# Spare TensorE products between the last key comparisons, with new weight homes, half-wise expert products and a new order of the first ticks

## The chip, the cores and the metric

The kernel runs on one core of one Trainium2 chip. The metric is device time in microseconds of one execution. Before the change three runs took 322.2, 322.96 and 324.96 us.

## The reference

The reference is a causal attention with a window of 128 positions and 4 sink positions (batch 4, 8 heads, 768 positions, head size 64), followed by a mixture of 8 experts with a capacity of 80 tokens each:

```
scores = q @ k.T / sqrt(64);  keep = sink | (0 <= i - j < 128)
x      = softmax(scores where keep) @ v            # 3072 rows of 512
logits = x @ w_gate;  expert = argmax;  gate = softmax(logits)[expert]
for e in range(8):
    tok = tokens of e; if more than 80: the 80 with the largest gate
    out[tok] = gate[tok] * (relu(x[tok] @ w1[e]) @ w2[e])   # w1 512x1024, w2 1024x512
```

All other rows of `out` are zero. All data is 32-bit floating point.

## The kernel before

**Attention.** A tick handles two units, each a pair of heads for one block of 128 queries. There are 48 ticks: four batches with 12 ticks each. In tick n the kernel issues the scores of tick n (`scores`, TensorE), masks and maxima (`softmax`, VectorE), the exponentials (`exps`, L541, ScalarE), and for tick n-1 the transposes of the probabilities (`transposes`), their copy out of PSUM (`keep_probs`, L569), the two masked copies on GpSimd (`own_probs`, `before_probs`), and for tick n-2 the weighted sums (`weighted`) and their copy (`keep_x`). The order on each engine is written out by hand: the loop calls these functions in a fixed order, and a calendar (`at`, `run`) adds further work at named places of a tick ("act mid", "pool", "dve end" and so on). The sink rows of `v` are rounded on ScalarE (`round_v`, L382) and the rest of the rounding is kept by GpSimd (`split_v`, L387); for batch 0 this happens in tick 1.

**Gate and ranks.** Each finished block of rows is turned, scaled and stored to `x_rows` in DRAM on the SP queue (L645; the last two on ScalarE's queue). Its gate gives one key for a token, and the kernel ranks tokens by comparing every key with all keys: VectorE compares pieces of 768 keys (`rank_compare`, L746 and L749), TensorE counts the columns of the results (`rank_count`, L763, and `rank_count_last`, L773). Comparisons that are left when attention ends run one after the other on VectorE. The column sums go through `owed` (L939), `off` (ScalarE), `ot` (GpSimd) and `os` (VectorE, L952). At the end `hot` (L983) marks the slots of the 80 tokens of each expert, 24 products give `pi` (L986), and the indices drive eight gathers from `x_rows` on GpSimd's DMA queue (L1007). Beside them TensorE runs 14 products of 480 columns into an unused bank (L1005).

**Experts.** For each expert the kernel transposes the gathered rows (`tokens`, L1037, copied by L1039), multiplies by w1 (`ffn1`, 128 products into `ph`, L1051), rectifies on ScalarE, multiplies by w2 (`ffn2`, 128 products into `py`, L1066), transposes back (`rows`, L1082) and scatters to `out`. The order is ffn1(0), ffn1(1), ffn2(0), ffn1(2), ffn2(1) and so on. In `ffn1` the four chunks c of the inner dimension run innermost, in `ffn2` the eight chunks k; a product addresses 64 columns of a weight tile (`columns`).

**Weights.** There are 32 weight tiles of 1024 KB, half a matrix each, loaded on the SP queue in the order of their use (`load_weight`, L293). The first 17 have homes of their own: NA = 6 loaded in ticks 26 to 41, every third tick; NB = 7 in the space of the q, k and v tiles (`ld`), which is closed after the last tick; NC = 4 in the space of the attention's working tiles (`wk`: probabilities, their copies, row blocks, comparison results). Tile 17 + k takes the home of tile 1 + 7k//4, so its load waits until the products of that tile are done. For the copies into unused output rows, `zeros` is written 24 times from tick 4 on.

Of the kernel before, what the change touches and what calls it, by code (L numbers as in the profile page):

```python
# [20 lines left out]
E, F = 8, 1024  # L21
# [211 lines left out]

Z0, ZD, W0, WD = 4, 1, 26, 3
NPB = NBLK // 2
NSPLIT = 1
SROWS = 16 * SINK
# [4 lines left out]
def attention_moe(ctx: ExitStack, tc, q, k, v, n_sink, window, w_gate, w1, w2, capacity, q_t, k_t, v_t, vs_t, wg_t, out):  # L244
# [4 lines left out]
    dram = ctx.enter_context(tc.tile_pool(name="dram", bufs=1, space=DRAM))  # L249
    fast = ctx.enter_context(ExitStack())  # L250

    NA, NB, NC = 6, 7, 4
    wpool = fast.enter_context(tc.tile_pool(name="wpool", bufs=NA))

    x_rows = dram.tile([NT, DM], F32, name="x_rows")
# [28 lines left out]
    def load_weight():  # L284
        n = len(wtiles)
        which, e, half = wsrc[n]
        src = (w1, w2)[which][e].rearrange("(g c p) f -> g p c f", g=2, p=P)[half]

        k = n - NA - NB - NC
        in_home.append(n if k < 0 else in_home[1 + 7 * k // 4])  # L290
        pool, m = homes[in_home[n]]
        t = pool.tile([P, 2 * F], F32, tag=f"w{m}", name=f"w_{which}_{e}_{half}", bufs=1)
        nc.sync.dma_start(t.rearrange("p (c f) -> p c f", c=src.shape[1]), src)  # L293
        wtiles[(which, e, half)] = t

    zeros = const.tile([P, DM], F32, name="zeros")
    ve.memset(zeros, 0.0)

    with ExitStack() as actx:
        wk = actx.enter_context(tc.tile_pool(name="wk", bufs=2))  # L300
# [54 lines left out]
        def load_q(g, pieces=1):  # L355
            qs[g] = ld.tile([P, NPAIR, 2 * P], F32, tag="q", name=f"q_{g}", bufs=3)
            n = NPAIR // pieces
            for i in range(pieces):
                nc.sync.dma_start(qs[g][:, i * n:(i + 1) * n], q_t[g // NPB, g % NPB][:, i * n:(i + 1) * n])

        def load_k(b, pieces=1):
            ks[b] = ld.tile([P, NPAIR, NBLK * BLKW], F32, tag="k", name=f"k_{b}")
            n = NPAIR // pieces
            for i in range(pieces):
                nc.sync.dma_start(ks[b][:, i * n:(i + 1) * n], k_t[b][:, i * n:(i + 1) * n])

        def load_v(b, upto=NPB):

            if b not in vv:
                vst[b] = vst_rows[b % 2]  # L370
                vv[b] = ld.tile([P, NBLK, DM], F32, tag="v", name=f"v_{b}")
# [8 lines left out]
        def round_v(b, m):  # L380
            a, hp = m // 2, slice(m % 2 * 2, m % 2 * 2 + 2)
            ac.copy(vst[b][0:SROWS, a, hp].bitcast(F32R), vst_raw[0:SROWS, a, hp])  # L382

        def split_v(b, m):

            a, hp = m // 2, slice(m % 2 * 2, m % 2 * 2 + 2)
            po.tensor_tensor(vst[b][32:SROWS, a, hp].bitcast(F32R), vst_raw[32:SROWS, a, hp], vst[b][32:SROWS, a, hp],  # L387
                             ALU.subtract)

        def scale_q(g, parts=1):  # L390
# [4 lines left out]


        first_q = qs[0] = ld.tile([P, NPAIR, 2 * P], F32, tag="q", name="q_0", bufs=3)
        first_k = ks[0] = ld.tile([P, NPAIR, NBLK * BLKW], F32, tag="k", name="k_0")
        for i in range(NPAIR):
            nc.sync.dma_start(first_q[:, i], q_t[0, 0][:, i])  # L400
            nc.sync.dma_start(first_k[:, i, 0:2 * BLKW], k_t[0][:, i, 0:2 * BLKW])
# [385 lines left out]
            at(Z0 + ZD * n, nc.sync.dma_start, out[n * P:(n + 1) * P, :], zeros)  # L787
        for n in range(NA):
            at(W0 + WD * n, load_weight)
        at((2, "pool"), make_experts)  # L790
        at((3, "pool"), make_picks)
        at((4, "pool"), make_ties)
# [3 lines left out]
        for b in range(B):  # L796
            s = b * NPB * NPAIR
            if b + 1 < B:
                at(s + 4, load_v, b + 1)
                at(s + 5, load_k, b + 1)  # L800
                for m in range(4):
                    at((s + 6 + m, "act end"), round_v, b + 1, m)
                    at((s + 7 + m, "pool"), split_v, b + 1, m)
        for m in range(4):
            at((1, "act mid"), round_v, 0, m)
            at((1, "pool"), split_v, 0, m)
        for g in range(2, NG):
            at((g - 2) * NPAIR + 1, load_q, g)
        for g in range(1, NG):
# [47 lines left out]
        with tc.manual_schedule():  # L857
            n = 0
            while n <= END:
                now[0] = n  # L860
                if n < NTK:
                    scores(n)
                t = n - 1 if 0 <= n - 1 < NTK else None
                if t is not None:
                    sink_probs(t)
                run(n, "dve early")
                run(n, "act early")
                if t is not None:
# [12 lines left out]
                run(n, "dve mid")  # L881
                if t is not None and n >= NTK:
                    own_probs(t)
                    before_probs(t)
                run(n, "pool")
                if t is not None:
                    if n < NTK:
                        own_probs(t)
                        before_probs(t)
                    sinks_keep(t)  # L890
                if 0 <= n - 2 < NTK:
                    weighted(n - 2)
                    keep_x(n - 2)
                run(n, "pe end")
                run(n, "act end")
                run(n, "dve end")
                run(n, "pool end")
                left = len(rank_todo)
                for _ in range(min(left, 3) if n >= NTK else -(-left // 3)):
                    rank_compare()  # L900
                run(n)
                if n == END:

                    lctx.close()
                    wpool2 = fast.enter_context(tc.tile_pool(name="wpool2", bufs=1, side="right", reuse_waits="tile"))
                    homes += [(wpool2, m) for m in range(NB)]
                    for _ in range(NB):
                        load_weight()
                n += 1

            now[0] = n
            i = NTILE - 1
# [44 lines left out]
            while rank_todo:  # L957
                rank_compare()
                rank_count_last(last)
            ve.tensor_tensor(colacc[:, 0:i], colacc[:, 0:i], last[:, 0:i], ALU.subtract)  # L960
            assert not cal and not rank_done, cal

    with ExitStack() as fctx:
# [77 lines left out]
        def ffn1(e):  # L1041
            need(0, e)
            x = xts.pop(e)
            h = wk.tile([P, HC, CAP], F32, tag="h", name=f"h_{e}")
            for half in range(2):
                ph = ps_h.tile([P, HC // 2, CAP], F32, tag="ph", name=f"ph_{e}_{half}")
                for f in range(HC // 2):
                    fc = half * (HC // 2) + f
                    for c in range(DC):
                        for m in range(2):  # L1050
                            pe.matmul(ph[m * D:(m + 1) * D, f], columns(0, e, c, fc * P + m * D),  # L1051
                                      x[:, c], start=(c == 0), stop=(c == DC - 1), skip_group_check=True)
                ac.activation(h[:, half * (HC // 2):(half + 1) * (HC // 2)], ph, AF.Relu)  # L1053
            hs[e] = h

        def ffn2(e, between=None):
            need(1, e)
            h = hs.pop(e)
            yts[e] = wk.tile([P, DC, CAP], F32, tag="yt", name=f"yt_{e}")
            py = ps_y.tile([P, DC, CAP], F32, tag="py", name=f"py_{e}")  # L1060
            last = ps_h.tile([P, HC // 2, CAP], F32, tag="ph", name=f"py2_{e}") if e == E - 1 else py
            for dc in range(DC):
                to = py if dc < DC // 2 else last
                for k in range(HC):
                    for m in range(2):
                        pe.matmul(to[m * D:(m + 1) * D, dc], columns(1, e, k, dc * P + m * D), h[:, k],  # L1066
                                  start=(k == 0), stop=(k == HC - 1), skip_group_check=True)
# [106 lines left out]
```

## Time and profile before

| what | value |
|---|---|
| runs | 322.2, 322.96, 324.96 us |
| profiled execution | 321.46 us, span 319.7 us |
| TensorE busy | 276.4 us (86%) |
| VectorE busy | 180.5 us (56%) |
| ScalarE busy | 159.1 us (50%) |
| GpSimd busy | 164.8 us (52%) |
| mean granted TensorE clock | 0.953 |
| DMA | 69.72 MB, mean 218 GB/s |
| weight loads | 32 of 1024 KB, median 6.7 us from issue to landing |

The span runs from the first to the last instruction of one profiled execution; the time of that execution is a little longer. Busy shares are averages over stages: the attention fills about the first 195 us, the last comparisons and the choice of tokens follow until about 222 us, the experts take the rest. The granted clock is the share of TensorE's full 2.4 GHz; 0.50 is 1.2 GHz.

### The profile page before, as it was taken

To read this page: it belongs to the slowest core of one execution; us is meant where nothing else is said; L and a number is where in the kernel's file an instruction comes from. 1 tells how busy PE (TensorE), PEld (TensorE's weight loads), DVE (VectorE), ACT (ScalarE), POOL (GpSimd) and SP (SyncE) were. 2 spreads that over 40 slices of the span, in tenths; PEclk is the share of its full clock that TensorE was granted. 3 is DMA by queue.
4 is the path that set the end of the run, shared out by engine and by line. 5 is a ranking of instruction groups with operands and counts; after the bars stand their busy time and mean duration, and the time that the engine had idled before them with its cause. 6 is when DMAs were issued, how large, how long until landed. Compare 5 with 4: busy or idle time off the path is not lost. (4 is left out here: it accounts for less than half of the span.)

```text
span 319.7 us, 11526 instructions
## 1 busy us (share of the span) xinstructions
PE 276.4 (86%) x4616; PEld 218.6 (68%) x4616; DVE 180.5 (56%) x576; ACT 159.1 (50%) x631; POOL 164.8 (52%) x365
## 2 busy tenths in 40 slices
PE   7498999999979999999999895745888989999792
PEld 2265776867767777777676673332788989998681
DVE  5345988777888989799989999970000000000001
ACT  0766897788968788777776661100111212111110
POOL 4396797769897588967667765507300111011001
PEclk9679999999999999999999999558999999999998
DMA  6999143699553899345260002999996696677501
GB/s 180 326 310 413 73 133 134 223 285 324 201 202 113 279 380 408 133 148 156 111 200 35 35 3 73 355 408 368 321 380 238 220 351 211 214 253 267 186 23 49
DMA packets 27115, 69.72 MB, mean 218 GB/s; under 512 B 2736, under 2 KB 3760, under 8 KB 26672
## 3 DMA queue, kind: packets, MB, share of 16 engines
q1 hardware_dynamic: 25744, 65.78, 59.5%
q0 software_dynamic: 1024, 2.62, 2.5%
q8 instruction: 38, 0.62, 0.8%
q10 hardware_dynamic: 288, 0.52, 0.4%
q14 instruction: 21, 0.17, 0.2%
HBM read 55.02 MB, written 13.89 MB: 216 GB/s over the span
## 5 line engine op out<-in xcount | busy, mean ns | idle before, releaser
L541 ACT ACTIVATE prob<-sc,nm 128x132 f32<-128x132 f32 (+1 forms) x192 | 69.0, 376 | 6.6 <-DVE nm L531 6.4
L504 PE MATMUL sc<-k,q 64*64 64x196 f32 (+2 forms) x768 | 48.4, 341 | 11.4 <-ACT prob L541 10.0
L1094 POOL DMA_INDIRECT out_dram<-y,idx x8 | 7.4, 921 | 81.8 <-ACT y L1083 71.6
L569 ACT COPY pt<-pp 128x512 f32<-128x512 f32 x48 | 28.1, 586 | 32.7 <-PE pp L557 24.1
L1039 DVE COPY xs<-px 128x320 f32<-128x320 f32 x8 | 3.9, 492 | 70.4 <-PE px L1037 70.4
L531 DVE TENSOR_REDUCE nm<-sc 128x2 f32<-128x264 f32 (+1 forms) x96 | 41.4, 431 | 3.3
L1051 PE MATMUL ph<-xs,w 128*64 128x80 f32 x1024 | 38.6, 233 | 5.2 <-issue 4.0
L524 DVE COPY_PREDICATED sc<-upper,sc 128x256 f32<-128x256 int8 x80 | 33.7, 421 | 14.0 <-PE sc L504 7.2
L504 PEld LDWEIGHTS sc<-k,q 64*64 64x64 f32 x768 | 21.6, 135 | 29.1 <-ACT prob L541 20.9
L1051 PEld LDWEIGHTS ph<-xs,w 128*64 128x64 f32 x1024 | 36.8, 137 | 6.4 <-issue 5.5
L1066 PE MATMUL py<-h,w 128*64 128x80 f32 x1024 | 38.4, 234 | 2.7 <-issue 2.0
L541 ACT ACTIVATION_READ_ACCUMULATOR prob<-sc,nm 128x1 f32 x192 | 40.3, 210 | 0.0
L1066 PEld LDWEIGHTS py<-h,w 128*64 128x64 f32 x1024 | 36.3, 137 | 4.9 <-issue 4.0
L598 PE MATMUL xp<-pt,v 128*64 128x128 f32 x384 | 37.5, 288 | 0.0
L577 POOL TENSOR_SCALAR_AFFINE_SELECT own<-pt 128x512 f32<-128x512 f32 (+1 forms) x48 | 28.7, 598 | 16.1 <-ACT pt L569 15.5
L749 DVE TENSOR_SCALAR_CACHE_REDUCE gt<-krow,keys 128x768 bf16<-128x768 f32 x36 | 35.5, 1004 | 0.0
L557 PE MATMUL pp<-ident,prob 128*128 128x128 f32 x192 | 32.3, 292 | 0.0
L598 PE MATMUL xp<-own,v 128*64 128x128 f32 x320 | 31.3, 274 | 0.0
L557 PEld LDWEIGHTS pp<-ident,prob 128*128 128x128 f32 x192 | 20.8, 144 | 13.9 <-issue 9.9
L1053 ACT ACTIVATE h<-ph 128x320 f32<-128x320 f32 x16 | 7.0, 438 | 44.1 <-PE ph L1051 44.1
L584 POOL TENSOR_SCALAR_AFFINE_SELECT pt<-pt 128x512 f32<-128x512 f32 (+1 forms) x48 | 27.2, 567 | 3.3
L641 POOL TENSOR_TENSOR xr<-xr,rs 128x512 f32<-128x512 f32 x24 | 25.6, 1069 | 6.0 <-ACT xr L636 5.7
(145 smaller groups left out, 461.6 us busy)
## 6 DMA issues: line engine op xcount, KB each, us to landing
w<-in_moe_w_dram SPq DMA_DIRECT2D x32, 1024.0 KB, 6.7
v<-in_v_t_dram SPq DMA_DIRECT2D x12, 512.0 KB, 7.5
out_dram<-zeros SPq DMA_DIRECT2D x24, 256.0 KB, 3.3
q<-in_q_t_dram SPq DMA_DIRECT2D x11, 512.0 KB, 7.2
x_rows<-xr SPq DMA_DIRECT2D x22, 256.0 KB, 2.2
k<-in_k_t_dram SPq DMA_DIRECT2D x3, 1584.0 KB, 9.0
k<-in_k_t_dram SPq DMA_DIRECT2D x1, 1056.0 KB, 9.7
vst_raw<-in_vs_t_dram SPq DMA_DIRECT2D x4, 256.0 KB, 6.2
```

Of the source, the lines that this page charges most:

```text
L504: pe.matmul(sc[u * D:(u + 1) * D, h, c0 + lo:c0 + hi], qs[g][r, hp, q0:q0 + D], ks[b][r, hp, k0 + lo:k0 + hi], start=True, stop=True, skip ...
L524: ve.copy_predicated(own, upper, sc[:, :, 0:P])
L531: ve.tensor_reduce(out=nm, in_=sc[:, :, lo_c:hi_c], axis=AX.X, op=ALU.max, negate=True)
L541: ac.activation(prob[:, a, h, p0:], sc[:, h, lo_c:hi_c], AF.Exp, bias=nm[:, h:h + 1], scale=1.0, accum_out=ssum[:, n, 2 * hp + h:2 * hp + ...
L557: pe.transpose(pp[:, a, h], prob[:, a, h, SINK:], ident)
L569: ac.copy(pt, st.pop((t, "pp")))
L577: po.affine_select(out=own[:, a0:], in_=pt[:, a0:], pattern=[[0, 2 - a0], [0, 2], [1, P]], compare_op=ALU.is_ge, fill=0.0, base=0, channel ...
L584: po.affine_select(out=pt[:, a0:], in_=pt[:, a0:], pattern=[[0, 2 - a0], [0, 2], [-1, P]], compare_op=ALU.is_gt, fill=0.0, base=0, channel ...
L598: pe.matmul(xp[h * D:(h + 1) * D, a * P:(a + 1) * P], val[:, (2 * hp + h) * D:(2 * hp + h + 1) * D], pr[:, a, h], start=False, stop=(a == ...
L749: ve.tensor_scalar(gt[:, 0:w], krow[:, c0:c0 + w], keys[:, i:i + 1], None, ALU.is_ge, ALU.add, accum_out=ra)
L1051: pe.matmul(ph[m * D:(m + 1) * D, f], columns(0, e, c, fc * P + m * D), x[:, c], start=(c == 0), stop=(c == DC - 1), skip_group_check=True)
L1066: pe.matmul(to[m * D:(m + 1) * D, dc], columns(1, e, k, dc * P + m * D), h[:, k], start=(k == 0), stop=(k == HC - 1), skip_group_check=True)
```

## The change

- One more weight tile has a home of its own (NA = 7), and these loads come every second tick from tick 26 on. Six tiles (NB) now lie in k/v tiles: k and v of a batch become one tile of a pool `kv` with two buffers. Three homes are a fifth such tile, loaded in ticks 40, 42 and 44; three are the tile of the last batch itself, two loaded in tick 47 and one after the last weighted sums, in the tick `END`. NC = 4 is as before.
- An exponential of one column of zeros is issued on ScalarE ahead of everything (`first_exp`).
- For batch 0, `round_v` and `split_v` run on VectorE at the end of tick 1.
- `keep_warm` issues products of 128x128 by 128x512 into a bank that nothing reads: one after each comparison of the loop over tile 22's rest, three after the small transposes, two after each of the last two comparisons, two more at the end.
- `ffn1` and `ffn2` (but for the last `ffn2`) run through all outputs with the first weight tile, then through all outputs with the second.
- The last expert's gathered rows go into `zeros`.

```
-Z0, ZD, W0, WD = 4, 1, 26, 3
+Z0, ZD, W0, WD = 4, 1, 26, 2
-    NA, NB, NC = 6, 7, 4
+    NA, NB, NC = 7, 6, 4
...
+    kv = fast.enter_context(tc.tile_pool(name="kv", bufs=2, side="right"))
+    kv_tiles = {}
+    def kv_homes(n):
+        t = kv_tiles[B - 1] if n else kv.tile([P, NPAIR * NBLK * BLKW + NBLK * DM], F32, tag="kv", name="wkv")
+        homes.extend((None, t[:, m * 2 * F:(m + 1) * 2 * F]) for m in range(NB // 2))
...
+    first_exp = const.tile([P, 1], F32, name="first_exp")
+    ac.activation(first_exp, zeros[:, 0:1], AF.Exp)
...
+        at((NTK - 1, "act early"), kv_homes, 1)
+        for _ in range(NB // 2 - 1):
+            at((NTK - 1, "act early"), load_weight)
+        W1 = (B - 1) * NPB * NPAIR + 4
+        at(W1, kv_homes, 0)
+        for n in range(NB // 2):
+            at(W1 + WD * n, load_weight)
...
-        for m in range(4):
-            at((1, "act mid"), round_v, 0, m)
-            at((1, "pool"), split_v, 0, m)
+        for m in (0, 2, 1, 3):
+            at((1, "dve end"), round_v, 0, m, ve.tensor_copy)
+            at((1, "dve end"), split_v, 0, m, ve)
...
                 run(n, "pe end")
+                if n == END:
+                    load_weight()
...
-                    wpool2 = fast.enter_context(tc.tile_pool(name="wpool2", bufs=1, side="right", reuse_waits="tile"))
-                    homes += [(wpool2, m) for m in range(NB)]
-                    for _ in range(NB):
-                        load_weight()
...
+            idle_bank = ps_m.tile([P, 512], F32, tag="m", name="idle_bank")
+            def keep_warm(times):
+                for _ in range(times):
+                    pe.matmul(idle_bank, ones_bf, pick_row[:, 0:4], start=True, stop=True)
...
             while rank_todo[0][0] < i:
                 rank_compare()
                 rank_count()
+                keep_warm(1)
...
                 pe.transpose(ct[:, m], crow[64:72, m * P:(m + 1) * P], ident[64:72, 64:72])
+            keep_warm(3)
...
             while rank_todo:
                 rank_compare()
                 rank_count_last(last)
+                keep_warm(2)
+            keep_warm(2)
...
-            xg[e] = sm.tile([CAP, DM], F32, name=f"xg_{e}")
+            xg[e] = sm.tile([CAP, DM], F32, name=f"xg_{e}") if e < E - 1 else zeros[0:CAP]
...
+            ph = [ps_h.tile([P, HC // 2, CAP], F32, tag="ph", name=f"ph_{e}_{half}") for half in range(2)]
+            for c0 in range(0, DC, DC // 2):
+                for fc in range(HC):
+                    for c in range(c0, c0 + DC // 2):
+                        for m in range(2):
+                            pe.matmul(ph[fc // (HC // 2)][m * D:(m + 1) * D, fc % (HC // 2)],
+                                      columns(0, e, c, fc * P + m * D), x[:, c],
+                                      start=(c == 0 and fc % (HC // 2) == 0), stop=(c == DC - 1), skip_group_check=True)
...
+            steps = [(dc, range(k0, k0 + HC // 2)) for k0 in (0, HC // 2) for dc in range(DC)]
+            if between is not None:
+                steps = [(dc, range(HC)) for dc in range(DC)]
+            for dc, some in steps:
```

## Rows read from the trace of the kernel before

**Rows 1.** The page, parts 1 and 2: TensorE's totals; granted clock, DMA share, 40 slices

```profile
PE 276.4 (86%) x4616; PEld 218.6 (68%) x4616; DVE 180.5 (56%) x576; ACT 159.1 (50%) x631; POOL 164.8 (52%) x365
...
PEclk9679999999999999999999999558999999999998
DMA  6999143699553899345260002999996696677501
```

**Rows 2.** Timeline, 2.5 to 17 us: start us, us, engine, line, operation [idle before]

```profile
2.58 1.65 DVE L347 CAST vst<-zeros 64x512 fp32r<-64x512 f32 x4
...
8.10 1.28 ACT L541 ACT_TABLE_LOAD   x1 [8.10 <-DVE nm L531]
...
10.30 1.59 PE L504 MATMUL sc<-k,q 64*64 64x64 f32 x16 [3.04 <-ACT prob L541]
...
12.97 0.59 ACT L569 COPY pt<-pp 128x512 f32<-128x512 f32 x1 [2.06 <-PE pp L557]
...
13.46 1.32 ACT L382 CAST vst<-vst_raw 64x256 fp32r<-64x256 f32 x4
...
14.68 0.36 ACT L541 ACTIVATE prob<-sc,nm 128x128 f32<-128x128 f32 x1
...
16.36 0.49 DVE L521 COPY_PREDICATED_SCALAR sc<-upper,negc 128x256 f32 x1 [3.17 <-ACT stt L565]
```

**Rows 3.** Windows: length; busy us of PE, PEld, DVE, ACT, POOL; clock; DMA; GB/s

```profile
10.00:20.30 10.30, 7.54 (x56) 4.53 (x56) 3.95 (x10) 6.32 (x30) 6.35 (x17) 0.50 1.04 361
...
201.20:218.30 17.10, 11.27 (x92) 6.54 (x92) 12.33 (x30) 0.97 (x4) 5.33 (x15) 0.50 1.03 390
...
215.60:218.30 2.70, 2.67 (x7) 1.28 (x7) 0.04 (x1) 0.00 (x0) 1.51 (x2) 0.50 1.02 394
218.40:220.00 1.60, 1.53 (x8) 0.66 (x6) 0.00 (x0) 0.00 (x0) 1.29 (x2) 1.00 1.05 389
...
222.80:243.00 20.20, 16.17 (x396) 14.87 (x398) 1.48 (x3) 1.75 (x4) 3.30 (x5) 1.00 0.98 333
...
264.00:285.00 21.00, 20.86 (x553) 20.02 (x551) 0.98 (x2) 4.40 (x9) 1.83 (x2) 1.00 0.68 220
```

**Rows 4.** The chain that ended last, in order of time: start us, us, what

```profile
214.25 0.74 PE pi L986 x8
...
216.49 6.25 DMA xg<-x_rows,idx_in
...
226.19 0.39 issue
...
226.99 0.34 issue
...
233.85 0.88 issue
234.74 2.02 PE ph L1051 x52
...
237.19 2.63 PE py L1066 x71
239.82 1.21 issue
...
260.36 0.83 issue
...
295.47 2.42 issue
```

**Rows 5.** Timeline of the last comparisons: VectorE's sum `os`

```profile
208.31 0.35 DVE L952 TENSOR_REDUCE os<-ot 128x24 f32<-128x192 f32 x1 [0.29 <-POOL ot L944]
```

**Rows 6.** Timeline of the SP queue, 196 to 300 us: the weight loads

```profile
198.22 96.82 SPq L293 DMA_DIRECT2D w<-in_moe_w_dram  x26
```

**Rows 7.** DMA issues, 303 to 320 us: count, median us to landing

```profile
out_dram<-y,idx POOLq DMA_INDIRECT x3, 2.6
```

**Rows 8.** The page, part 3: packets, MB, share of the instruction queue

```profile
q8 instruction: 38, 0.62, 0.8%
```

More of the change, by code (lines that the diff above doesn't have):

```diff
@@ L291, in load_weight @@
         pool, m = homes[in_home[n]]
-        t = pool.tile([P, 2 * F], F32, tag=f"w{m}", name=f"w_{which}_{e}_{half}", bufs=1)
+        if pool is None:
+            t = m
+        else:
+            t = pool.tile([P, 2 * F], F32, tag=f"w{m}", name=f"w_{which}_{e}_{half}", bufs=1)
         nc.sync.dma_start(t.rearrange("p (c f) -> p c f", c=src.shape[1]), src)
         wtiles[(which, e, half)] = t
+    kv = fast.enter_context(tc.tile_pool(name="kv", bufs=2, side="right"))
[3 more added lines that the diff above has]
+        homes.extend((None, t[:, m * 2 * F:(m + 1) * 2 * F]) for m in range(NB // 2))
     zeros = const.tile([P, DM], F32, name="zeros")
     ve.memset(zeros, 0.0)
+    first_exp = const.tile([P, 1], F32, name="first_exp")
+    ac.activation(first_exp, zeros[:, 0:1], AF.Exp)
     with ExitStack() as actx:
@@ L359, in load_q, with alloc_kv @@
                 nc.sync.dma_start(qs[g][:, i * n:(i + 1) * n], q_t[g // NPB, g % NPB][:, i * n:(i + 1) * n])
+        def alloc_kv(b):
+            if b not in ks:
+                t = kv.tile([P, NPAIR * NBLK * BLKW + NBLK * DM], F32, tag="kv", name=f"kv_{b}")
+                kv_tiles[b] = t
+                ks[b] = t[:, 0:NPAIR * NBLK * BLKW].rearrange("p (h c) -> p h c", h=NPAIR)
+                vv[b] = t[:, NPAIR * NBLK * BLKW:].rearrange("p (c f) -> p c f", c=NBLK)
         def load_k(b, pieces=1):
-            ks[b] = ld.tile([P, NPAIR, NBLK * BLKW], F32, tag="k", name=f"k_{b}")
+            alloc_kv(b)
             n = NPAIR // pieces
@@ L367, in load_v @@
         def load_v(b, upto=NPB):
-            if b not in vv:
+            if b not in vst:
                 vst[b] = vst_rows[b % 2]
-                vv[b] = ld.tile([P, NBLK, DM], F32, tag="v", name=f"v_{b}")
+                alloc_kv(b)
             for i in range(v_done.get(b, 0), upto):
@@ L378, in attention_moe, with round_v, split_v @@
         v_done = {}
-        def round_v(b, m):
+        def round_v(b, m, copy=ac.copy):
             a, hp = m // 2, slice(m % 2 * 2, m % 2 * 2 + 2)
-            ac.copy(vst[b][0:SROWS, a, hp].bitcast(F32R), vst_raw[0:SROWS, a, hp])
-        def split_v(b, m):
+            copy(vst[b][0:SROWS, a, hp].bitcast(F32R), vst_raw[0:SROWS, a, hp])
+        def split_v(b, m, eng=po):
             a, hp = m // 2, slice(m % 2 * 2, m % 2 * 2 + 2)
-            po.tensor_tensor(vst[b][32:SROWS, a, hp].bitcast(F32R), vst_raw[32:SROWS, a, hp], vst[b][32:SROWS, a, hp],
+            eng.tensor_tensor(vst[b][32:SROWS, a, hp].bitcast(F32R), vst_raw[32:SROWS, a, hp], vst[b][32:SROWS, a, hp],
                              ALU.subtract)
@@ L397, in attention_moe @@
         first_q = qs[0] = ld.tile([P, NPAIR, 2 * P], F32, tag="q", name="q_0", bufs=3)
-        first_k = ks[0] = ld.tile([P, NPAIR, NBLK * BLKW], F32, tag="k", name="k_0")
+        alloc_kv(0)
+        first_k = ks[0]
         for i in range(NPAIR):
@@ L1044, in ffn1 @@
             h = wk.tile([P, HC, CAP], F32, tag="h", name=f"h_{e}")
-            for half in range(2):
[L1046 to L1053, printed above, removed]
+            ph = [ps_h.tile([P, HC // 2, CAP], F32, tag="ph", name=f"ph_{e}_{half}") for half in range(2)]
[6 more added lines that the diff above has]
+                                      start=(c == 0 and fc % (HC // 2) == 0), stop=(c == DC - 1), skip_group_check=True)
+            for half in range(2):
+                ac.activation(h[:, half * (HC // 2):(half + 1) * (HC // 2)], ph[half], AF.Relu)
             hs[e] = h
@@ L1061, in ffn2 @@
             last = ps_h.tile([P, HC // 2, CAP], F32, tag="ph", name=f"py2_{e}") if e == E - 1 else py
-            for dc in range(DC):
+            steps = [(dc, range(k0, k0 + HC // 2)) for k0 in (0, HC // 2) for dc in range(DC)]
+            if between is not None:
+                steps = [(dc, range(HC)) for dc in range(DC)]
+            for dc, some in steps:
                 to = py if dc < DC // 2 else last
-                for k in range(HC):
+                for k in some:
                     for m in range(2):
                         pe.matmul(to[m * D:(m + 1) * D, dc], columns(1, e, k, dc * P + m * D), h[:, k],
-                                  start=(k == 0), stop=(k == HC - 1), skip_group_check=True)
+                                  start=(k == 0 and (between is not None or dc == 0)), stop=(k == HC - 1),
+                                  skip_group_check=True)
                 if dc == DC // 2 - 1 and between is not None:
```

## The prediction

> **What bounds the kernel now.** I read the page first. TensorE has the largest busy share, 276.4 us, but its granted clock drops in two places, and the line of the DMA engines shows four stretches: nearly full early on, almost nothing between 168 and 192 us, full from 200 to 240 us, about two thirds after that [rows 1]. So there are stages with different limits, and I took them one by one.
>
> The timeline of the first ticks shows a serial start. The first exponentials wait for a table load of 1.28 us that begins only when the first maxima are there; the scores of tick 1 wait for ScalarE; then four rounding copies (1.32 us) stand between a copy of tick 1 and its exponentials, so VectorE waits 3.17 us for tick 2 [rows 2]. All this runs at the lower granted clock, 0.50, which is 1.2 GHz, from 10 to 20.3 us [rows 3].
>
> The chain of waits begins only at the last comparisons (VectorE), goes through the ranks, the last 8 products of `pi`, one gather of 6.25 us, and then the experts on TensorE. In the expert stage it holds pieces called "issue", in which nothing that the profile shows is waited for: 0.39, 0.34, 0.88 and 1.21 us before 243 us, then 0.83 and 2.42 us [rows 4]. The windows show the same loss: 396 products in 20.2 us at the start of the experts, 553 in 21.0 us later [rows 3]. In the last comparisons TensorE has the granted clock 0.50 over 17.1 us and is busy for 11.27 us of them; VectorE, with 12.33 us there and the chain on it, sets the pace.
>
> **First ticks.** The early `first_exp` moves the table load into the 8.10 us in which ScalarE is idle. That is worth at most 1.28 us; the second unit of tick 0 must still wait for its own maximum, so I take 1.1. Without the rounding copies, ScalarE's next exponentials follow the copy that ends at 12.97 + 0.59 = 13.56 instead of starting at 14.68: another 1.12 us. But VectorE takes over the work at the end of tick 1: four casts (a 64x512 cast took 1.65 / 4 = 0.41 us [rows 2]; half the width, about 0.25) and four subtractions (no row of that shape on VectorE; between 0.25 and 0.41, I take 0.33), together 2.3 us. Its gap before 16.36 began at 16.36 - 3.17 = 13.19; 1.1 earlier is 12.1, and 2.3 of work ends at 14.4. So VectorE ends last and the gain is 16.36 - 14.4 = 2.0 us, not the 2.2 that ScalarE would allow. Behind VectorE's new work stand only the maxima of tick 2, counted here; GpSimd loses four subtractions and its next masks come sooner. Denser work may keep the clock up: half of TensorE's 7.54 busy us before 20.3 [rows 3] is 3.8, about half of it on the path, so 0 to 2; I take 0.8, because an idle gap of TensorE remains at tick 1. Sum **2.8 us**, ends 0.9 (VectorE's 2.3 us eats all but the table) and 4.4. The attention behind it is a steady pipeline, so a head start should last.
>
> **Weight loads of the attention stage.** One load more in ticks 26 to 38, three in ticks 40 to 44, two in tick 47, one in the tick `END`. The six that are new between 150 and 200 us lie where the DMA line shows between 0 and 6 tenths [rows 1]; the buffers of the three in ticks 40 to 44 belong to batch 2, which is finished two ticks before. The two in tick 47 make SP wait for the scores just issued, and the one in `END` for the last weighted sums. Behind them on SP is a store of finished rows, wanted only by the gather some 20 us later. Cost: nothing; if that cover went, a store late by a load (2.7 us: 1.05 MB at the 390 GB/s of [rows 3]) would still be in time.
>
> **Spare products between comparisons.** Fifteen products of 128x512: one behind each of six comparisons, three behind the small transposes, then two, two and two. The nearest rows are the warm-up products of 480 columns: 2.67 / 7 = 0.38 us at 0.50, 1.53 / 8 = 0.19 us at 1.00 [rows 3]. So 0.41 or 0.20 us each, 6.2 or 3.1 us in all, against 17.1 - 11.27 = 5.8 us of idle TensorE. The comparisons stay on VectorE and gain nothing. What can be gained: the last 8 products of `pi` (0.74 us at 0.50 [rows 4], 0.37 at full clock), and part of the 0.29 us for which VectorE waits on the sums [rows 5]. What can be lost: the spare products stand ahead of real ones in TensorE's order; at the lower clock one product (0.41) and a backlog of about 0.5 would delay the sums and with them VectorE, 0.9 us. I take a gain of **0.3 us** (ends: 1.0 gained, 0.9 lost), nearest to the `pi` row.
>
> **The gather.** Before, 26 loads stand on SP from 198.22 on [rows 6], eleven of them ready to go, so the gather at 216.49 shares the DMA engines with them. Now seven of those eleven homes become four: three of the four new tiles lie over probabilities and row blocks that are done before the comparisons end; the fourth lies over two comparison buffers and must wait for them. Some six loads of 2.7 us are then over before the gather is issued, the seventh perhaps at the same time. A scatter of the same 80 rows without weight traffic landed in 2.6 us [rows 7]. I take 2.85 for the gather: **3.4 us**, ends 0 and 3.65.
>
> **The experts.** What are the stops? Between those at 233.85 and 239.82 lie 52 + 71 products and a transpose of four: 127, with their weight loads 254 instructions [rows 4]. The queue called "instruction" moved 38 packets [rows 8] for 2 x 4616 instructions of TensorE [rows 1], 243 to a packet. So TensorE seems to stop where a packet of its instructions is late behind weight data. The pair at 226 us, a few products apart, does not fit this and stays unexplained.
> The Trainium skill, Runtime: NRT & Kernel Launch, section Instruction fetch mechanics, says that the next block is fetched by the sequencer's own DMA queue and that the cost of crossing into it is mostly hidden. By that rule the stops would have another cause and would stay (rival two); the stops of up to 2.42 us speak against "mostly hidden" where weights are being loaded.
> At the later pace (21.0 / 553 = 38.0 ns), 396 products are 15.0 us; 5.2 are lost. About 1.2 of it, a copy between transposes and products for the first two experts, stays. The rest, 2.82 of stops and 1.2 of slower pace, goes if the weights are there: 4.0. Later, the buffers named by 1 + 7k//4 come free in pairs (8 with 9, 22 with 23), so two loads start together, and the stops of 0.83 and 2.42 follow such pairs. With the halves the even tile is free half a block earlier and the pairs come apart; but the loads of single tiles now start in mid-block. I take half of 3.25: 1.6. Sum **5.6 us**, ends 2.5 and 7.8. The order by halves costs no instruction; each rectifier pass is hidden by the next expert's products.
>
> **Sum.** 2.8 + 0.3 + 3.4 + 5.6 = 12.1. The profiled execution took 321.46 us (span 319.7); 321.46 - 12.1 = 309.4. The median of the runs is 1.5 above it; I place the forecast near the middle, **310.0**.
>
> **Rivals.** One, the DMA engines stay full (0.12): if the four following loads all wait for the comparison buffers, 4 x 2.7 = 10.8 us of loading starts near the end of the comparisons and runs over the gather; 3.4 and about half of the 4.0 are lost: 315.4. For it: they share one SP queue in order; against: three lie over tiles done early.
> Two, the stops have another cause (0.10): 2.82 and 1.6 stay, 314.4. For it: the unexplained pair; against: the spacing.
> Three, the spare products don't raise the clock (0.07): the sums come 0.9 late, the 14 warm-up products run slowly and hold the first transposes by some 0.4: 310 + 0.3 + 0.9 + 0.4 = 311.6. For it: TensorE at 11.27 of 17.1 us did not raise it.
> Four, slower (0.03): in mid-block loads meet each of the some 16 instruction packets of the experts. The mean of the four stops that fit is 1.34; 16 x 1.34 = 21.4 in place of 6.07. Without the stops the other gains are 12.1 - 2.82 - 1.6 = 7.7, so this decides from (7.7 + 6.07) / 16 = 0.86 us each; at 1.34 the time is 321.46 + 21.4 - 6.07 - 7.7 = 329.1. Against: from 264 to 285 us loads run and TensorE is busy for 20.86 of 21.0 us.
>
> **Numbers.** My forecast has 0.68. Its ends combine to about 304.5; on the other side the range reaches over rivals one to three, to 317. Within 1% (3.2 us, about what a measurement tells from no change) needs most of the gains gone at once: 0.04; slower 0.03; faster 0.93.
>
> **What would show it.** Tick 3's scores start two to four us earlier; granted clock 1.00 before `pi`, its last 8 near 0.4 us; first gather under 3.5 us; no "issue" over 0.5 us before the third expert; no stop over 1 us later. The forecast fails if the gather still takes 6 us, or if stops appear at each packet.

## The result, and the profile after

The changed kernel took 318.44 us (median of 20 runs, 314.81 to 321.33) beside 322.04 us for the kernel before (20 runs, 319.01 to 324.96): ratio 0.9878, 95% interval 0.985 to 0.9905. Ratios leave out executions more than 1.5% above the fastest of their kernel; medians take all. The gain is 3.6 us; 12 were forecast, and the time lies outside the range. The profiled execution took 317.12 us (span 315.3), so against the 321.46 us of before there are 4.34 us to account for.

The page: TensorE's totals, granted clock and DMA share in 40 slices, the instruction queue.

```profile
PE 280.6 (89%) x4629; PEld 222.1 (70%) x4631; DVE 183.9 (58%) x584; ACT 157.9 (50%) x628; POOL 161.9 (51%) x361
...
PEclk9759999999999999999999999697899999999997
DMA  6999134599572899983825382983357696878601
...
q8 instruction: 38, 0.62, 0.8%
```

Against [rows 1] the new homes are plain: the DMA engines now load weights between 150 and 190 us, and from 213 to 229 us they are busy to three tenths, where they were full. But the slice from 221 to 229 us with 8 tenths of clock, at the start of the experts, is new.

The chain that ended last, in order of time (start us, us, what):

```profile
214.22 0.49 PE pi L1025 x8
...
215.35 4.68 PE warm L1044 x14
220.03 0.28 PE px L1076 x4
...
220.94 1.71 PE ph L1090 x43
...
223.06 0.36 issue
...
224.48 1.07 issue
225.55 0.37 PE ph L1090 x4
...
226.99 4.10 PE ph L1090 x72
...
268.38 0.22 issue
...
273.24 0.19 issue
```

The `DMA xg` step of 6.25 us [rows 4] is gone from the chain; 14 warm-up products stand in its place. From the second expert on the stops of 0.88, 1.21, 0.83 and 2.42 us [rows 4] have become 0.22 and 0.19 in this execution. But the first expert, which nobody expected to suffer, now runs in bursts of one to four products with stops of up to 1.07 us between them. Windows of the same execution (length; busy us of PE, PEld, DVE, ACT, POOL; clock; DMA; GB/s):

```profile
10.00:20.30 10.30, 6.95 (x57) 4.21 (x55) 7.75 (x19) 4.74 (x21) 4.89 (x14) 0.57 1.04 374
11.40:25.10 13.70, 11.40 (x89) 7.73 (x90) 8.81 (x21) 6.00 (x29) 8.10 (x20) 0.50 1.04 358
...
206.00:216.20 10.20, 6.83 (x92) 4.28 (x92) 7.05 (x18) 0.97 (x4) 1.44 (x3) 1.00 0.66 243
215.30:220.10 4.80, 4.75 (x18) 2.48 (x17) 0.06 (x1) 0.00 (x0) 3.59 (x4) 0.64 0.25 71
220.90:231.10 10.20, 7.36 (x129) 6.37 (x130) 0.00 (x0) 0.44 (x1) 4.24 (x6) 0.83 0.29 82
243.00:264.00 21.00, 21.00 (x560) 20.31 (x558) 0.98 (x2) 3.96 (x8) 1.88 (x2) 1.00 0.77 246
```

Read beside [rows 3]: the last comparisons end at full clock, as forecast, yet it falls again under the warm-up products; the first expert has 0.29 of DMA share, so its stops are not weights; later 560 products fill 21.0 us, with not one idle moment. The first ticks, timeline:

```profile
0.80 1.28 ACT L311 ACT_TABLE_LOAD   x1 [0.80 <-PEq L1181]
...
11.62 1.64 PE L526 MATMUL sc<-kv,q 64*64 64x64 f32 x16 [1.27 <-ACT prob L563]
...
12.02 0.29 DVE L403 CAST vst<-vst_raw 64x256 fp32r<-64x256 f32 x1 [1.07 <-DMA vst_raw<-in_vs_t_dram]
...
13.87 1.14 DVE L408 TENSOR_TENSOR vst<-vst_raw,vst 32x256 fp32r<-32x256 f32 x1
...
15.58 0.57 DVE L408 TENSOR_TENSOR vst<-vst_raw,vst 32x256 fp32r<-32x256 f32 x1
16.18 0.49 DVE L543 COPY_PREDICATED_SCALAR sc<-upper,negc 128x256 f32 x1
```

Tick 2's scores come at 11.62 us, in place of 15.53. VectorE then waits 1.07 us for the sink rows, spends 4.1 us on the eight rounding operations (12.02 to 16.15), and reaches tick 2 at 16.18 us: it was 16.36 [rows 2]. The clock is 0.50 for 13.7 us, not 10.3. By tick 12 nothing is left: 51.79 us in both traces.

Where the 4.34 us come from, in the two profiled executions:

| stretch | before | after | gain |
|---|---|---|---|
| to the end of the last comparison | 210.62 | 210.60 | 0.02 |
| to the end of `pi` | 4.36 | 4.10 | 0.26 |
| to the issue of the first gather | 1.51 | 0.89 | 0.62 |
| the gather | 6.25 | 3.24 | 3.01 |
| landing to first transposes | 0.04 | 1.04 | -1.00 |
| to the first expert's products | 1.13 | 1.07 | 0.06 |
| the first expert's 128 products | 6.08 | 10.15 | -4.07 |
| to the last product | 82.81 | 77.00 | 5.81 |
| to the end of the execution | 8.66 | 9.03 | -0.37 |

### The profile page after: what moved, and what is told of

It reads as the page before. It is cut to its first block, busy times and chain, and to the rows that moved or that the text cites. A ratio compares the mean times of both kernels' runs of the same rounds, so it can differ in the third digit from the quotient of the medians.

```text
span 315.3 us, 11553 instructions
## 1 busy us (share of the span) xinstructions
PE 280.6 (89%) x4629; PEld 222.1 (70%) x4631; DVE 183.9 (58%) x584; ACT 157.9 (50%) x628; POOL 161.9 (51%) x361
## 5 line engine op out<-in xcount | busy, mean ns | idle before, releaser
L526 PE MATMUL sc<-kv,q 64*64 64x196 f32 (+2 forms) x768 | 49.0, 344 | 10.8 <-ACT prob L563 9.5
L526 PEld LDWEIGHTS sc<-kv,q 64*64 64x64 f32 x768 | 21.9, 136 | 28.2 <-ACT prob L563 21.4
L620 PE MATMUL xp<-pt,kv 128*64 128x128 f32 x384 | 37.9, 291 | 0.0
L1090 PE MATMUL ph<-xs,w 128*64 128x80 f32 x704 | 28.8, 240 | 4.2 <-issue 3.6
L620 PE MATMUL xp<-own,kv 128*64 128x128 f32 x320 | 31.6, 276 | 0.0
L1090 PEld LDWEIGHTS ph<-xs,w 128*64 128x64 f32 x704 | 26.9, 143 | 5.7 <-issue 4.8
L785 PE MATMUL bank_t<-gt,pick_row 128*128 128x384 bf16 (+2 forms) x92 | 22.7, 335 | 2.7 <-DVE gt L771 2.7
L1111 PE MATMUL py<-h,w 128*64 128x80 f32 x640 | 24.5, 234 | 0.2 <-issue 0.2
## 6 DMA issues: line engine op xcount, KB each, us to landing
kv<-in_v_t_dram SPq DMA_DIRECT2D x12, 512.0 KB, 10.1
```

Source lines behind the costliest of these rows:

```text
L526: pe.matmul(sc[u * D:(u + 1) * D, h, c0 + lo:c0 + hi], qs[g][r, hp, q0:q0 + D], ks[b][r, hp, k0 + lo:k0 + hi], start=True, stop=True, skip ...
L620: pe.matmul(xp[h * D:(h + 1) * D, a * P:(a + 1) * P], val[:, (2 * hp + h) * D:(2 * hp + h + 1) * D], pr[:, a, h], start=False, stop=(a == ...
L1090: pe.matmul(ph[fc // (HC // 2)][m * D:(m + 1) * D, fc % (HC // 2)], columns(0, e, c, fc * P + m * D), x[:, c], start=(c == 0 and fc % (HC ...
```

## The experiments

Theory at the start: the terms of the sum hold one by one, and the loss sits in the first expert. Rivals: it comes from the rounding, from the halves or from the spare products. Each set below ran on one chip, beside the kernel before.

**Set A**, before at 321.16 us: one part taken out of the changed kernel at a time.

Without the spare products:
```
-                for _ in range(times):
+                for _ in range(0):
```


> The changed kernel without the fifteen spare products; everything else as changed (its median 318.4 us). Forecast: they are worth 0.3 us, so 318.7. Theory A (what the trace of the changed kernel suggests): they raise the clock for the choice of tokens, but it falls again to 0.50 at about 216 us, so they buy only the 0.25 us of the last products of pi; without them the clock stays at 0.50 until the 14 warm-up products raise it near 218 us: the last 8 products of pi take 0.74 instead of 0.49 us, time 318.2 to 318.9. Rival B: by raising the clock early they let it fall at the wrong moment; without them the clock is full when the experts begin and the time is lower by 1 us or more, 317.4 or less.

312.35 us (311.0 to 313.59), ratio 0.9735 [0.9699, 0.9771].

Without `first_exp`, with the rounding where it was:
```
-    first_exp = const.tile([P, 1], F32, name="first_exp")
-    ac.activation(first_exp, zeros[:, 0:1], AF.Exp)
...
-        for m in (0, 2, 1, 3):
-            at((1, "dve end"), round_v, 0, m, ve.tensor_copy)
-            at((1, "dve end"), split_v, 0, m, ve)
+        for m in range(4):
+            at((1, "act mid"), round_v, 0, m)
+            at((1, "pool"), split_v, 0, m)
```


> The changed kernel without the early exponential and with the rounding for batch 0 back on ScalarE and GpSimd. Forecast: 2.8 us lost, 321.2. Theory A: the gain of the first ticks depends on how long the clock stays at 0.50 at the start; in the one trace it stayed 3.4 us longer than before and the ticks after the sixth start at the same time as before, so on the mean of many runs it is worth 0 to 1.5 us: 318.4 to 319.9. Rival B: the table load alone (1.1 us) stays as gain: 319.5.

313.08 us (309.84 to 314.06), 0.9738 [0.9695, 0.9781].

With the old order of products:
```
-            for c0 in range(0, DC, DC // 2):
...
-            steps = [(dc, range(k0, k0 + HC // 2)) for k0 in (0, HC // 2) for dc in range(DC)]
...
```


> The changed kernel with ffn1 and ffn2 in the order of before (all chunks of one output, then the next output). Forecast: the halves are worth 1.6 us by pulling the paired loads apart; without them stops of about 0.8 and 2.4 us come back late in the experts: 320.0. Rival B: the weights come early enough either way and the paired loads cost nothing any more: 318.4, no stop over 0.5 us after the third expert. The stops in the first expert's products (0.36 to 1.07 us, 222 to 227 us) should stay in both.

315.71 us (313.3 to 319.27), 0.9838 [0.9802, 0.9873].

With the old homes and load times:
```
-Z0, ZD, W0, WD = 4, 1, 26, 2
+Z0, ZD, W0, WD = 4, 1, 26, 3
...
-    NA, NB, NC = 7, 6, 4
+    NA, NB, NC = 6, 7, 4
...
```


> The changed kernel with the weight homes and load times of before (six early, seven after the last tick, four more). Forecast: the gather takes about 6 us again (3.4 us more) and the start of the experts loses 4.0: 325.8. Theory A: with the late gather the first expert begins when GpSimd has few gathers left, so its stops (3.4 us in the changed kernel) shrink to below 1 us, and the net loss is 4 us: about 322.5. Rival B: no difference within 1 us, 317.4 to 319.4: the gain of the change came from the halves.

318.1 us (314.47 to 320.9), 0.9865 [0.9814, 0.9915]. Three of the four are well below the 318.44 us of the whole change, and in none does the first expert stop: 4.65 us for its 128 products. So no one part that was taken out is the cause. (The whole change did not run in this set, so the set prices no part.) What a part undoes its trace shows: with the old homes the chain (start us, us, what) has the long gather and the stops back,

```profile
215.39 6.14 DMA xg<-x_rows,idx_in
...
236.11 0.83 issue
...
291.40 2.15 issue
```

and with the old order three stops of 4.1 us together are in the chain:

```profile
254.72 0.51 issue
265.03 0.99 issue
286.07 2.64 issue
```

**Set B**, before at 323.13 us: is it the kernel, or the set of runs? First the changed kernel again, unaltered.

> The changed kernel itself once more, beside its variants on one chip. If the four kernels that each lacked one part (312.4, 313.1, 315.7, 318.1 us) are faster because of what they lack, this gives 317.5 to 319 us and its trace has the stops in the first expert's products again (some 3 us between 222 and 227). If the difference lay in the chip or the hour, it gives 312 to 314 and no such stops.

313.06 us (310.66 to 314.41), 0.9712 [0.9658, 0.9766]: 10.1 us below the kernel before. Its first expert, timeline of TensorE:

```profile
218.50 0.44 PE L1076 MATMUL px<-ident,xg 80*128 80x80 f32 x4
219.57 4.65 PE L1090 MATMUL ph<-xs,w 128*64 128x80 f32 x128 [0.63 <-issue]
```

Then one more spare product, which moves all later instructions by one:
```
-            keep_warm(2)
+            keep_warm(3)
```


> The changed kernel with sixteen spare products instead of fifteen: the last group has three. By its work this is worth nothing (0.2 us at most, under VectorE's marking of slots). Theory P: the stops in the first expert's products come from where TensorE's instruction packets begin and end in the stream, so a shift by one product and one weight load moves or removes them, and the time differs from the changed kernel by more than 1 us (below 317.4). Rival: the stops come from the spare products themselves, the time stays within 1 us of 318.4 and the stops stay.

313.05 us (311.0 to 315.62, and one run of 506.41), 0.9683 [0.9625, 0.9741]: no difference. As this chip has no stops, the run can't tell whether the shift would move them.

Without `first_exp` alone (`-    ac.activation(first_exp, ...)`):

> The changed kernel without the early exponential; the rounding stays on VectorE. Forecast: the table load of 1.28 us comes back on the path, about 1 us slower than the changed kernel (319.4). Rival: what made the kernel without both first-tick edits faster (313.1) is this instruction: then about 313 and no stops in the first expert.

314.79 us (310.57 to 315.12, and one run of 431.88), 0.9716 [0.9649, 0.9783]: its worth of about a microsecond is not resolved.

With the rounding alone back on ScalarE and GpSimd (the last six lines of the second diff):

> The changed kernel with the rounding for batch 0 back on ScalarE and GpSimd; the early exponential stays. If VectorE's eight operations (4.1 us in tick 1 in the changed kernel's trace, instead of the 2.3 forecast) are the cost, this is 1 to 2 us faster than the changed kernel; if the stops in the first expert hang on what the engines did some 200 us earlier, they are gone and it is about 313; otherwise 318.

309.97 us (308.43 to 311.91), 0.9615 [0.9561, 0.967]: 3.1 us faster than the changed kernel, and the fastest of all. Since every kernel of sets A and B runs its first expert beside the same gathers without a stop, I then took the gathers for innocent. That was too early.

**Set C**, another chip, before at 322.26 us.

> The changed kernel once more, unaltered. Its 20 first runs gave a median of 318.44 us with stops in the first expert (10.15 us for 128 products); a later set gave 313.06 us without them (4.65 us). Theory one, the stops belong to a set of runs and not to the kernel: 311 to 315 us, first expert 4.6 to 4.7 us. Theory two, 313 was the exception: 317 to 320 us, and stops of 0.36 to 1.07 us in the first expert.

319.04 us (315.08 to 322.01), 0.9903 [0.9864, 0.9942], and the stops are there again: 10.10 us for the 128 products. They belong to the chip or to where the program lies on it, not to the code alone.

> The kernel before, unaltered, with a trace of its own. Theory one (as above): 319.5 to 323.8 us, and the two stops of 0.38 and 0.34 us in the first expert of its first trace are either gone or elsewhere, while the stops of 0.8 to 2.5 us behind pairs of weight loads stay (within 1 us of 0.88 + 1.21 + 0.83 + 2.42 = 5.3 us in all). Theory two: the same stops in the same places.

322.51 us. The stops of 0.83, 0.83 and 2.59 us stay; the pair in the first expert is gone, which ran at the granted clock 0.50 for most of its 7.33 us.

The gathers 2 to 7 held back until the first expert's products are done:
```
+        for e in range(2):
+            gather(e)
...
+            if e == 0:
+                held = sm.tile([P, 1], F32, name="held")
+                po.tensor_copy(held, hs[0][:, HC - 1, 0:1])
+                for n in range(2, E):
+                    gather(n)
```


> The gathers of the experts 2 to 7 are issued only when the first expert's first products are done, so that GpSimd issues no gathers beside the first expert. If the stops in the first expert come from these gathers, it has none even where the unaltered kernel of this call has them, and is then 5 us faster than that one. If they don't, it is within 1.5 us of the unaltered kernel; the rows of expert 2 are wanted some 9 us later, when they have landed.

320.09 us, 0.9921 [0.988, 0.9961]: no gain, but the trace tells why. TensorE, then GpSimd:

```profile
218.44 4.65 PE L1093 MATMUL ph<-xs,w 128*64 128x80 f32 x128 [0.63 <-issue]
...
224.09 2.71 PE L1093 MATMUL ph<-xs,w 128*64 128x80 f32 x62 [0.58 <-DVE xs L1081]
227.11 0.42 PE L1093 MATMUL ph<-xs,w 128*64 128x80 f32 x5 [0.30 <-issue]
...
230.01 0.37 PE L1093 MATMUL ph<-xs,w 128*64 128x80 f32 x4 [1.08 <-issue]
...
232.87 2.43 PE L1093 MATMUL ph<-xs,w 128*64 128x80 f32 x33 [0.87 <-issue]
```

```profile
224.35 1.01 POOL L1046 DMA_INDIRECT xg<-x_rows,idx_in  x1 [0.54 <-issue]
...
230.73 0.96 POOL L1046 DMA_INDIRECT zeros<-x_rows,idx_in  x1 [0.30 <-issue]
```

The first expert is clean, and the stops have gone with the gathers into the second. On a chip that has the stops they come from the gathers.

The rounding back, and 4 warm-up products in place of 14 (`-            for _ in range(14):`, `+            for _ in range(4):`):

> The changed kernel with the rounding of tick 1 back on ScalarE and GpSimd, and with 4 warm-up products instead of 14. The 14 took 4.68 us at the granted clock 0.50 and ended 1 us after the first gather landed. Theory one, they hold the first transposes: with 4 (about 1.4 us) the transposes start within 0.2 us of the landing, 0.9 us earlier than in the version that has only the rounding back (309.97 us): about 309. Rival: TensorE idles some 1.8 us ahead of the transposes, the granted clock falls to 0.50 in the first expert, whose 4.65 us become up to 9: 312 to 314 us.

315.5 us (314.44 to 319.38), 0.981 [0.9756, 0.9865]. Both theories are right in part: the transposes start 0.04 us after the landing, but the clock stays at 0.50 until 221.1 us, and the first 56 products take 3.36 us, where 48 took 2.11 in the unaltered kernel. The warm-up's 1.0 us can't be had this way. The first expert has its stops here too. Why the time is 3.5 us below the unaltered kernel's stays open: the first gather is issued at 213.82 us here, but at 215.68 and 213.09 in the two traces of this set that have VectorE's rounding.

**Set D**, a third chip, before at 322.4 us.

> The changed kernel, unaltered, as the measure for the three others of this call. On one chip it took 313.06 us without stops in the first expert, on another 319.04 us with them. Either value says which kind of chip this is: 311 to 315 us with 4.6 to 4.7 us for the first 128 products, or 317 to 320 us with about 10 us.

316.33 us (315.65 to 318.13), 0.9837 [0.9806, 0.9869], first expert 10.10 us: a chip with stops.

Data or issuing? The gathers 1 to 7 skip every row beyond the first 384, and GpSimd fills six of their tiles with zeros beforehand, so this kernel leaves out most rows of seven experts:
```
+            if 0 < e < E - 1:
+                po.memset(xg[e], 0.0)
...
-                                  bounds_check=NT - 1, oob_is_err=False)
+                                  bounds_check=NT - 1 if e < 1 else NT // 8 - 1, oob_is_err=False)
```


> The gathers of the experts 1 to 7 skip every row beyond the first 384, so GpSimd issues them as before and about an eighth of their bytes moves; the experts 1 to 7 then work partly on zeros. Where the unaltered kernel has stops in the first expert: if the moved data cause them, this one has none or few and is 4 to 6 us faster; if the issuing by GpSimd causes them, they stay and the time is within 1.5 us of the unaltered kernel. Where the unaltered kernel has none, both theories give the same time.

319.2 us, 0.9886 [0.9849, 0.9923]. The gather queue moved (packets, MB, share of 16 engines, from 216 to 226 us) only

```profile
q0 software_dynamic: 498, 0.30, 11.1%
```

against 505 packets and 1.28 MB in the unaltered kernel from 215 to 225 us, and TensorE's stops are the same:

```profile
219.22 2.17 PE L1092 MATMUL ph<-xs,w 128*64 128x80 f32 x50 [0.63 <-issue]
222.42 0.38 PE L1092 MATMUL ph<-xs,w 128*64 128x80 f32 x4 [1.03 <-issue]
...
225.28 3.92 PE L1092 MATMUL ph<-xs,w 128*64 128x80 f32 x69 [1.07 <-issue]
```

Not the data, then: the packets or their issuing. (That the time is 2.9 us above the unaltered kernel, where at most 1.5 was expected, stays open; its first expert took 9.97 us, and the six fills, 0.52 us each on GpSimd, are a second difference that no run prices.) The Trainium skill, DMA: Bandwidth & Descriptors, section Terms, says that for GpSimd's transfers the descriptors are written into rings in SBUF, while for the other queues they go to the engines directly. The run agrees in that the stops don't depend on the bytes; none shows how such writes would hold TensorE's instructions.

Nor are these stops late packets of instructions, which the prediction took the later ones for. In the profiled execution of the first 20, from 211 to 228 us, these queues moved data (packets, MB, share of 16 engines):

```profile
q0 software_dynamic: 512, 1.31, 27.3%
q1 hardware_dynamic: 500, 0.99, 15.3%
```

The instruction queue is not among them: one of its packets ended at 210.54 us and the next began at 228.09, when the stops were over (226.99 us).

Only two gathers at once, each further one behind an expert of its own:
```
...
+            if e + 2 < E:
+                held = sm.tile([P, 1], F32, name=f"held_{e}")
+                po.tensor_copy(held, hs[e][:, HC - 1, 0:1])
+                gather(e + 2)
```


> Only the gathers 0 and 1 are issued at once; gather e + 2 is issued when the first products of expert e are done, so each stands alone, some 9 us apart. Theory: TensorE holds work for about 2 us (46 to 62 products ran before the first stop), a single gather lasts 1.3 us, so no stop is left: first expert 4.65 us, no stop over 0.4 us in the second, and the time is 4.5 to 6 us below the unaltered kernel where that has stops, within 1 us of it where it has none. Rival, each gather costs its own stop of about 1 us wherever it lies: at most 1 us is gained.

314.53 us (313.41 to 317.27), 0.9773 [0.9736, 0.9811]: 1.8 us below the unaltered kernel, not 4.5. The first expert takes 4.65 us, but gather 2 now meets weight loads, and the chain holds it:

```profile
226.93 6.75 DMA xg<-x_rows,idx_in
...
246.30 0.29 issue
246.97 0.34 issue
```

The same with the rounding back:

> As the kernel with spread gathers, and the rounding of tick 1 back on ScalarE and GpSimd. That rounding was worth 3.1 us (309.97 against 313.06). If both effects add: 310 to 311 us with or without stops in the unaltered kernel. If the rounding's gain depends on something else of that chip, it equals the spread version within 1 us.

314.88 us (312.83 to 317.9), 0.9772 [0.973, 0.9814]: here the rounding is worth nothing.

**Set E**, a fourth chip, before at 320.73 us. Three gathers at once, gather e + 3 behind expert e, the rounding back (`-        for e in range(2):`, `+        for e in range(3):`, and 3 for 2 in the block above):

> Gathers 0, 1 and 2 at once, gather e + 3 when the first products of expert e are done; the rounding of tick 1 is back on ScalarE and GpSimd. In the spread version gather 2 took 6.75 us beside weight loads and TensorE waited 0.7 to 2.4 us for it; here it lands before the first expert starts, so that wait goes. The pairs of stops of 0.3 us behind each later gather and scatter stay where the chip has them. On such a chip 314.88 - 1 = about 314; on one without stops about 310, within 1 us of the rounding alone (309.97).

314.11 us (310.55 to 316.68), 0.9737 [0.9677, 0.9797]. The rounding alone back:

> The rounding of tick 1 alone back on ScalarE and GpSimd; all eight gathers at once. It took 309.97 us on a chip without stops in the first expert. On a chip with them, theory one (the stops come from GpSimd's gathers): 4 to 6 us more, 314 to 316, and the kernel with spread gathers of this call is 1 to 4 us below it. Rival (the chip's difference lies elsewhere): both kernels within 1 us of each other.

317.98 us (315.62 to 321.14), 0.9874 [0.9815, 0.9932], first expert 11.09 us. So 3.9 us lie between all gathers at once, beside the first expert, and gathers three at once and then singly; by its own median the second is above the 314 to 316 expected. With three at once, TensorE and GpSimd:

```profile
219.11 4.65 PE L1093 MATMUL ph<-xs,w 128*64 128x80 f32 x128 [0.63 <-issue]
...
242.13 0.41 PE L1114 MATMUL py<-h,wkv 128*64 128x80 f32 x5 [0.32 <-issue]
242.86 2.50 PE L1114 MATMUL py<-h,wkv 128*64 128x80 f32 x66 [0.32 <-issue]
```

```profile
225.02 1.01 POOL L1046 DMA_INDIRECT xg<-x_rows,idx_in  x1 [0.54 <-issue]
...
240.12 0.98 POOL L1046 DMA_INDIRECT xg<-x_rows,idx_in  x1 [0.54 <-DVE xs L1081]
241.41 0.96 POOL L1143 DMA_INDIRECT out_dram<-y,idx  x1 [0.30 <-issue]
```

The gather at 225.02, alone, stops nothing. The one at 240.12 has a scatter 1.29 us behind it, and two stops of 0.32 us follow.

## Why the prediction was wrong

**The first expert, inside the term "experts".** This step failed most: 4.07 us lost where about 1.4 were to be gained. I wrote that the pair of stops at 226 us [rows 4] "does not fit this and stays unexplained", and counted it to stops that go once weights are there. It was another thing: TensorE stops while GpSimd issues indirect transfers (gathers or scatters by an index) back to back (eight of them, 1.27 us apart, 215.59 to 225.67 us). Before, the gather of 6.25 us kept the first expert away until 7.4 us after the first issue, so only the last gathers met it. With the gather at 3.24 us it starts 5.35 us after, in the middle of them. What the gather gained (3.01 us) was given back there and more. The stops showed in four sets of runs of the six, with the first 20 as one.

**The rest of the experts.** Right in kind: 5.81 us measured from the end of the first expert on, where the forecast had 5.6 with the first expert in it, so about 4.2 without. In the unaltered kernel without stops the first expert gives 1.43 and the rest 3.84: 5.3. That these stops are late instruction packets (rival two denied it) the traces show: at all four stops of before from 233.85 us on, TensorE goes on 1.3 to 1.4 us after a packet of the instruction queue has ended (the last: packet from 295.55 to 296.54 us, TensorE at 297.89), and so it does behind the 0.22 and 0.19 us of after. The packets took 0.96 to 1.24 us each, so they were late in starting. That weights hold them is argued, not shown; it agrees with the run that undoes the homes. The sign "no stop over 1 us later" held in the first profile alone: the three other traces of the unaltered kernel have one such stop each, of 1.70, 1.23 and 1.01 us. For the halves it is less plain: with the old order the ratio is 0.9838 and not 0.9712, but a stop of 1.70 us at 286 us stayed in that execution of the unaltered kernel too, where the old order has 2.64. The Trainium skill, Runtime: NRT & Kernel Launch, section Instruction fetch mechanics, calls the cost of crossing a block mostly hidden. The stops of 0.22 and 0.19 us agree with that, the 2.15 and 2.64 us of the kernels with old homes or old order do not.

**The gather.** Right: 3.0 us, forecast 3.4; and 0.62 more in front of it, which I had not seen. But I named no successor for that wait. The 14 warm-up products, 4.68 us and mostly at the lower clock, end 1.0 us after the landing. Rival three had this term at 0.4, tied to a clock that does not rise; it rose, and fell again.

**First ticks.** Mis-sized: 2.8 forecast, nothing measured in this execution. VectorE's eight operations took 4.1 us and not 2.3 (one subtraction 1.14, against 0.33 taken). They began when forecast, at 12.02 us for 12.1: VectorE was ready at 10.94, but the input came 1.07 us later. And the clock stayed low longer: tick 3's scores still start 2.4 us earlier, as forecast (18.02 for 20.41 us), tick 4's only 0.2 (23.01 for 23.24). The lower end, 0.9, did not allow for the clock. In the two traces of before tick 12 starts at 51.8 and 51.6 us. In eleven other traces with VectorE's rounding, tick 12 starts between 49.1 and 52.0 us: at 49.1 to 50.2 where the low stretch lasts 10.3 us or less (50.7 without `first_exp`), at 50.8 to 52.0 where it lasts 13.6 or 13.7. With the rounding back and `first_exp` kept it is 50.3 to 50.9 in all five, so `first_exp` alone gives about the 1.1 us taken for it, and the 2.0 us taken for the new order are borne out (1.4 to 2.6) by the five traces with both in which the low stretch lasts 10.3 us or less. On one chip the rounding cost 3.1 us, on another nothing; its mean worth stays open.

**Spare products.** Right: 0.26 us, forecast 0.3, and `pi` at 0.49 per eight. In whole runs it does not show (0.9735 without them, 0.9712 with, on two chips). **Weight loads of the attention**: cost nothing, as forecast.

On the one chip without the stops that ran the unaltered kernel the time was 313.06 us, inside the range and 3 above the forecast; its trace has the first ticks (tick 12 at 50.80 us), the warm-up products and the late stop of 1.70 us against it. With the stops it was 316.33 to 319.04 us in the three sets that ran it, so the same forecast lies inside or outside its range by the chip. What stays open is why two of the chips don't have them: GpSimd issues at the same pace there (1.27 us) and the gathers' packets take as long, and where a program and its data lie in memory could not be chosen.

## What to carry to other kernels

A stop that a theory of all other stops does not cover is worth its own question: price what happens if it grows. When a wait gets shorter, look at what runs beside the work that now starts earlier; here a burst of gathers, once hidden behind the first of them, came to lie under the first products, and issuing only as many as are needed at once gave back 3.9 us on one chip (three at once) and 1.8 us on another (two). And one set of runs on one chip can hide an effect of 5 us that a second chip shows.

## What the runs showed of the hardware

Indirect transfers issued by GpSimd 1.3 us apart stop TensorE's instructions on some chips: after some 46 to 62 products, bursts of 1 to 5 products with stops of 0.3 to 1.08 us, whether 1.28 MB or 0.30 MB moves; 128 products then take 10 to 11 us in place of 4.65. No packet of the instruction queue moves beside these stops in the profile after. Single transfers, 5 us or more from the next, stopped nothing. On two chips none of it showed (on one the unaltered kernel ran, on the other four variants). And after such a slow stretch the granted clock fell to 0.50 (226.5 to 229.9 us in the profile after), so the loss goes on when the stops are over. Another kind of stop is a late instruction packet: in the traces of before and after TensorE goes on 1.3 to 1.4 us after the packet has ended.
